# Window attention with a convolutional position term: a hand-ordered pipeline, interleaved convolution, 64x64 score tiles, GpSimd norms and a shared transposed buffer

## The chip, the cores and the metric

One core of one Trainium2 chip. The metric is device time in microseconds (us) of one execution. Both kernels give the reference's result within tolerance.

TensorE is called PE here, its weight loads PEld, VectorE DVE, ScalarE ACT, GpSimd POOL, and SyncE, which issues transfers, SP. "Clock" is the mean clock that the throttle granted to PE, 1.0 being full speed.

## The reference, cut to what matters

```python
# x: (1, 511, 511, 192) bf16; 7x7 windows: 73 x 73 = 5329 windows of 49 tokens; 4 heads of 48
pe = depthwise 3x3 convolution of x with dw_pe (per channel)
x0 = x + pe
h  = layernorm(x0)                       # no scale, no shift
qkv = windows(h) @ w_qkv                 # 192 -> 576
attn = softmax(q k^T * 48**-0.5)         # per window and head, 49 x 49
out = (attn v) @ w_o
return x0 + unwindow(out)
```

## The kernel before

Windows are taken in blocks of 128, one window to a partition (42 blocks), and within a block in 16 groups of 8 windows. The convolution treats one channel of a block as one matmul: the 81 pixels of the padded 9x9 patch are the contraction rows, the 128 windows the output partitions, the 49 tokens the columns. So a block has 192 convolution matmuls of 49 columns.

```python
def conv_tile(blk, it):                       # 20 channels in one tile of two PSUM banks, out of 4 tiles
    ps = PS.next()
    for cc in range(ncn):
        nc.tensor.matmul(ps[:, col : col + S], lhsT=XP[0:KP, :, c], rhs=T[0:KP, c, :], start=True, stop=True)
    nc.vector.tensor_tensor(out=xc[...], in0=ps..., in1=xc[...], op=ALU.add)      # x was loaded into xc
# ... (statistics with bn_stats, one token at a time; reciprocal root on DVE)
def transposes(blk):                          # layer norm's scale is folded into the transposing matmul
    D = Dcur.pop((blk, g))                    # ident * rstd, built on POOL
    nc.tensor.matmul(ps[0:KT, ...], lhsT=xc[:, s0 + ss, kt * KT : (kt + 1) * KT], rhs=D[:, ss, :], ...)
def stage_B(g):                               # scores: q holds both heads of a pair beside zeros
    for jj in range(4):
        for ab in range(2):
            for wp in range(2):
                nc.tensor.matmul(ps[64 * wp : 64 * wp + 64, col : col + 2 * S],
                    lhsT=k_[:, ab, w * S : w * S + 64], rhs=q_[:, ab, w, :, :]..., tile_position=(0, 64 * wp))
def proj(blk):
    # ... two matmuls of OT with Wo, then in every second tile the residual as an identity matmul:
    nc.tensor.matmul(ps[:, col : col + C], lhsT=ident[:], rhs=xc[:, s0 + ss, :], start=False, stop=True)
for g in range(NGL + LE + 1):                 # schedule of one group
    if ck == 0: transposes(blk)               # all 98 at once, at the start of a block
    stage_B(g - 1); stage_D(g - 2)
    if ck == LE: proj(blk - 1); store(blk - 1); load_xc(blk + 1)       # whole projection at once
    stage_E(g - 3)
    if ck >= CONV0: conv_tile(nb, ...)        # three tiles of 20 channels in one run, in four groups
    if ck == cend: load_xp(nb + 1)
    stage_A(g)                                # q, k, v of the group
```

KP is 81, KT 96 (half the channels), S 49. Stage A is q, k and v, B the scores and the exponential, D the weighted sum, E the transposition of its result.

## Time and profile before

Before: 5347.09 us (median of 2 runs, 5326.14 to 5368.04).

| | busy | share |
|---|---|---|
| PE | 4490 us | 84% |
| DVE | 3817 us | 72% |
| ACT | 2745 us | 51% |
| POOL | 758 us | 14% |
| granted clock | | 0.824 |

### The profile page before, as it was taken

How to read it: one execution, taken by the hardware profiler on the slowest of the kernel's cores; microseconds unless marked ns; L12 is line 12 of the kernel's file. 1: busy time of each engine (PE TensorE's matmuls, PEld its weight loads, DVE VectorE, ACT ScalarE, POOL GpSimd, SP SyncE). 2: the span in 40 equal slices, each digit the busy share in tenths (PEclk: the TensorE clock that was granted, in tenths of full speed). 3: DMA queues.
4: the chain of work that ended last, by engine and by line, in shares of the span. 5: the costliest groups of instructions: out<-in, count | busy, mean ns of one | idle time of the engine just before them, and what ended most of it. 6: DMA issues, size and time to landing. Idle time of an engine off the chain costs nothing.

```text
span 5337.2 us, 148265 instructions
## 1 busy us (share of the span) xinstructions
PE 4490.1 (84%) x65427; PEld 3661.5 (69%) x65427; DVE 3816.7 (72%) x6912; ACT 2744.5 (51%) x3385; POOL 758.0 (14%) x833
## 2 busy tenths in 40 slices
PE   2788888888888888888988888888888888888887
PEld 1666676667776676677776777767666776677776
DVE  6776777767776777777677777777777777767776
ACT  1554555545555555555555455555555555545555
POOL 1111111111111111111111111111111111111120
PEclk9887888887778887888788877788888888877888
DMA  6554445554455555554455544455555445544431
GB/s 67 51 75 70 68 71 80 82 73 68 68 68 70 71 72 74 71 74 71 68 73 91 75 68 68 68 72 72 74 72 72 73 70 78 85 74 67 68 48 32
DMA packets 512613, 375.27 MB, mean 70 GB/s; under 512 B 453129, under 2 KB 453321, under 8 KB 511958
## 3 DMA queue, kind: packets, MB, share of 16 engines
q1 hardware_dynamic: 480918, 265.08, 38.1%
q0 software_dynamic: 30592, 100.32, 10.6%
q8 instruction: 514, 8.42, 0.7%
q14 instruction: 141, 1.16, 0.1%
q10 hardware_dynamic: 448, 0.30, 0.0%
HBM read 265.31 MB, written 100.27 MB: 68 GB/s over the span
## 4 chain that ended last, share of the span: by engine, by line
PE 44%; DVE 16%; ACT 14%; DMA 12%; SPq 9%; issue 4%; POOL 1%; DVEq 0%; ACTq 0%; POOLq 0%
PE ps L412 12%; PE ps L282 8%; SPq L396 7%; DMA out_dram<-XC 7%; PE ps L369 6%; DMA XC<-in_x_dram 5%; PE ps L453 5%; PE ps L532 4%; DVE kT L424 4%; ACT hT L355 4%; DVE Qb L422 3%; PE ps L431 2%; DVE XC L284 2%; PE ps L560 2%; ACT kT L426 2%
## 5 line engine op out<-in xcount | busy, mean ns | idle before, releaser
L412 PE MATMUL ps<-hT,Wqk 96*128 96x392 bf16 x5336 | 1233.5, 380 | 76.7 <-DVE XC L284 62.2
L478 ACT ACTIVATE PT<-ps 128x784 bf16<-128x784 f32 x667 | 552.7, 829 | 1095.3 <-PE ps L453 1080.3
L421 ACT CAST Qb<-ps 64x784 bf16<-64x784 f32 x667 | 555.3, 833 | 657.5 <-PE ps L412 655.7
L412 PEld LDWEIGHTS <-Wqk 96*128 96x128 bf16 x5336 | 529.4, 108 | 486.1 <-issue 252.5
L284 DVE TENSOR_TENSOR XC<-ps,XC 128x980 bf16<-128x980 f32 x378 | 437.9, 1176 | 503.0 <-PE ps L282 247.2
L282 PE MATMUL ps<-T,XP 81*128 81x49 bf16 x8064 | 744.0, 264 | 55.5 <-DMA XP<-in_x_dram 55.5
L567 ACT CAST OT<-ps 96x784 bf16<-96x784 f32 x667 | 541.0, 811 | 456.0 <-PE ps L560 452.4
L282 PEld LDWEIGHTS <-XP 81*128 81x128 bf16 x8064 | 733.9, 220 | 57.6 <-issue 55.5
L431 PE MATMUL ps<-Wv,hT 96*128 96x192 bf16 x5336 | 663.5, 277 | 16.4 <-DVE On L544 9.0
L532 PE MATMUL ps<-V,PT 49*64 49x49 bf16 x21344 | 542.5, 195 | 159.1 <-DVE Qb L422 81.2
L431 PEld LDWEIGHTS <-hT 96*128 96x128 bf16 x5336 | 548.8, 111 | 180.0 <-issue 91.6
L544 DVE TENSOR_TENSOR On<-ps,rs 128x768 bf16<-128x768 f32 x667 | 634.6, 951 | 16.0
L532 PEld LDWEIGHTS <-PT 49*64 49x64 bf16 x21344 | 466.2, 116 | 260.4 <-issue 217.7
L327 POOL TENSOR_TENSOR D<-ident,rstd 128x896 bf16<-128x896 bf16 x294 | 486.2, 1681 | 1074.8 <-DVE rstd L320 1053.3
L424 DVE CAST kT<-ps 128x784 bf16<-128x784 f32 x462 | 450.0, 974 | 219.2 <-PE ps L412 209.1
L304 DVE BATCH_NORM_STATS2 bnst<-XC 128x6 f32<-128x192 bf16 x2058 | 600.5, 343 | 0.2
L453 PE MATMUL ps<-Qb,kT 128*64 128x98 bf16 x10672 | 408.0, 225 | 180.7 <-DVE Qb L422 132.2
L422 DVE CAST Qb<-ps 64x784 bf16<-64x784 f32 x462 | 451.6, 978 | 110.6 <-ACT Qb L421 100.1
L355 ACT CAST hT<-ps 96x896 bf16<-96x896 f32 x462 | 452.4, 1109 | 135.9 <-PE ps L346 134.9
L560 PE MATMUL ps<-ident,On 128*96 128x98 bf16 x5336 | 412.1, 226 | 114.4 <-DVE kT L424 110.9
L453 PEld LDWEIGHTS <-kT 128*64 128x64 bf16 x10672 | 341.5, 121 | 231.5 <-issue 131.7
L108 POOL DMA_DIRECT2D XC<-in_x_dram x386 | 216.0, 560 | 1865.9 <-DVE rs L543 996.3
(73 smaller groups left out, 4396.2 us busy)
## 6 DMA issues: line engine op xcount, KB each, us to landing
XC<-in_x_dram POOLq DMA_DIRECT2D x277, 294.0 KB, 7.5
out_dram<-XC SPq DMA_DIRECT2D x277, 294.0 KB
XP<-in_x_dram SPq DMA_DIRECT2D x210, 246.4 KB
XP<-in_x_dram SPq DMA_DIRECT2D x68, 243.0 KB
XC<-in_x_dram POOLq DMA_DIRECT2D x37, 165.4 KB, 7.1
out_dram<-XC SPq DMA_DIRECT2D x37, 165.4 KB
XP<-in_x_dram SPq DMA_DIRECT2D x22, 216.0 KB
XP<-in_x_dram SPq DMA_DIRECT2D x18, 212.6 KB
```

What stands on the lines that cost most here:

```text
L282: nc.tensor.matmul(ps[:, col : col + S], lhsT=XP[0:KP, :, c], rhs=T[0:KP, c, :], start=True, stop=True)
L304: nc.vector.bn_stats(out=bnst[:, s, :], in_=xc[:, s, :])
L355: nc.scalar.copy(out=hv[0:KT, kt, :, s0 : s0 + NDG], in_=src)
L412: nc.tensor.matmul(ps[:, ab * 512 : ab * 512 + TOK], lhsT=Wqk[kt][0:KT, which * 2 + ab, :], rhs=hT[0:KT, kt, ck * CH : (ck + 1) * CH, 0:S] ...
L421: nc.scalar.copy(out=dst[0:64, :, :, 0, :], in_=src[0:64])
L422: (nc.vector.tensor_copy if dve_help else nc.scalar.copy)(out=dst[64:128, :, :, 1, :], in_=src[64:128])
L424: nc.vector.tensor_copy(out=dst[:, :, 0:TOK], in_=two_bank(ps, TOK))
L431: nc.tensor.matmul(ps[:, col : col + C], lhsT=hT[0:KT, kt, ck * CH + 2 * jj : ck * CH + 2 * jj + 2, :].rearrange("p w s -> p (w s)"), rhs= ...
L453: nc.tensor.matmul(ps[64 * wp : 64 * wp + 64, col : col + 2 * S], lhsT=k_[:, ab, w * S : w * S + 64], rhs=q_[:, ab, w, :, :].rearrange("p ...
L478: nc.scalar.activation(out=pt[:, 0 : 16 * S].rearrange("p (b n) -> p b n", b=2), in_=two_bank(ps, 8 * S), func=ACTF.Exp, scale=scale,)
L532: nc.tensor.matmul(ps[64 * wp : 64 * wp + 64, col : col + S], lhsT=pt[64 * wp : 64 * wp + S, pc_ : pc_ + 64], rhs=v_[64 * wp : 64 * wp + S ...
L544: nc.vector.tensor_tensor(out=o_[:].rearrange("p (b j) (h d) -> p b (j h) d", b=2, d=DH), in0=ov[:, :, :, 0:DH], in1=r_[:].rearrange("p (b ...
```

## The change: intent and diff

The intent is to keep PE fed: no stage runs in a burst. The convolution is spread, a matmul or two after each long one, and is meant to hide its weight load there. Scores use four 64x64 tiles and q needs no zeros. Layer norm is applied ahead on GpSimd, so the transposes are plain; the residual too goes to GpSimd. The transposed norm (hT) and the transposed attention output (OT) share one buffer HO. The rows of x no longer sit in a buffer ahead of the convolution, but come in two small row buffers, on SP's queue. The core of a 1,367-line diff:

```diff
-    PS = _Rot([psum.tile([128, 1024], F32, name=f"ps{i}") for i in range(4)])
+    self.PS = _Rot([psum.tile([128, 1024], F32, name=f"ps{i}") for i in range(3)])
+    self.PE_ = psum.tile([128, 512], F32, name="pse")      # attention's transposes
+    self.PC = psum.tile([128, 512], F32, name="psc")       # convolution: ONE bank
 # ... convolution
-    ps = PS.next()                                         # 20 channels, then one add
+    PCB = self.PC
+    mm(PCB[:, (c % 10) * S : (c % 10 + 1) * S], lhsT=XP[0:KP, :, c], rhs=T[0:KP, c, :], ...)
+    if cv.c % 10 == 0 or cv.c == C:
+        nc.vector.tensor_copy(out=self.X[cv.b % 3][:, :, c0 : c0 + n], in_=PCB[...])
 # ... after each long matmul
+    def fill():
+        quota[0] += (conv_goal - conv_start) / nlong
+        while n and quota[0] >= 0.999 and conv.c < conv_goal:
+            quota[0] -= 1.0
+            conv_mm(conv)
 # ... x rows, norm, transposes
-    nc.gpsimd.dma_start(out=xc[...], in_=xw[...])          # whole block, POOL's queue
+    nc.sync.dma_start(out=t[p]..., in_=dram(x, *at))       # one of seven rows, SP's queue, two buffers
+    nc.gpsimd.tensor_tensor(out=hbuf(b)[:, s0:s1, :], in0=self.X[b % 3][:, s0:s1, :], in1=rstd..., op=ALU.mult)
+    for kt in range(2):                                    # both halves in ONE PSUM tile
+        for i in range(N): mm(pb[0:KT, kt * 1024 + i * 128 : ...], lhsT=h[...], rhs=ident[:], is_transpose=True)
+        eng = nc.vector.tensor_copy if kt == 0 else nc.scalar.copy
+        eng(out=HO[b % 2][0:KT, kt, :, s0 : s0 + N], in_=pb[0:KT, kt * 1024 : ...])
 # ... scores
-    nc.tensor.matmul(ps[...], lhsT=k_[:, ab, ...], rhs=q_[:, ab, w, :, :], tile_position=(0, 64 * wp))
+    mm(ps[...], lhsT=k_[64 * hp : 64 * hp + DH, ab, ...], rhs=q_[64 * hp : 64 * hp + DH, ab, ...], tile_position=(64 * hp, 64 * cp))
 # ... residual
-    nc.tensor.matmul(ps[...], lhsT=ident[:], rhs=xc[:, s0 + ss, :], start=False, stop=True)
+    nc.gpsimd.tensor_tensor(out=xv, in0=xv, in1=o[:, 0:n, :], op=ALU.add)
 # ... reload of the patches
+    if conv.c == C and xp_due:
+        load_xp(b + 2)
```

## The prediction

> **What bounds the kernel now.** I read the busy table, the costliest groups, the timeline of one block of 128 windows, the same block by stretches, and the DMA issues.

> ```profile
> PE 4490.1 (84%) x65427; PEld 3661.5 (69%) x65427; DVE 3816.7 (72%) x6912; ACT 2744.5 (51%) x3385; POOL 758.0 (14%) x833
> ...
> PEclk9887888887778887888788877788888888877888
> ```

> PE is the busiest engine, but its clock is granted at about 0.8, so "busy" holds slow time too. The stretches of one block (non-convolution steps, convolution steps, the next steps) show where; the columns are length, then busy time of PE, PEld, DVE, ACT, POOL, then the clock:

> ```profile
> 2016.00:2063.00 47.00, 40.12 (x695) 33.17 (x694) 36.41 (x44) 26.43 (x34) 4.42 (x8) 1.00 0.71 117
> 2064.00:2104.00 40.00, 38.98 (x419) 32.13 (x419) 22.95 (x27) 7.21 (x9) 1.00 (x4) 0.50 0.18 28
> ```

> Here the clock is full outside the convolution and half within it. The timeline of PE (start, length, operation) says what that costs:

> ```profile
> 2018.36 1.54 PE L412 MATMUL ps<-hT,Wqk 96*128 96x392 bf16 x8
> ...
> 2087.58 5.50 PE L282 MATMUL ps<-T,XP 81*128 81x49 bf16 x60
> 2092.91 2.79 PE L412 MATMUL ps<-hT,Wqk 96*128 96x392 bf16 x8
> ```

> The same eight q/k projections take 1.54 us at full clock and 2.79 us beside the convolution; 60 convolution matmuls take 5.50 us, 90 ns each (start to start also 90 ns in the few that ran at full clock[...]). A block takes (5337-157)/41.7 = 124 us, 157 us being where the first projection starts and 41.7 = 667 groups of 8 windows / 16.

> Groups that the sums below use (mean ns before the bar):

> ```profile
> L304 DVE BATCH_NORM_STATS2 bnst<-XC 128x6 f32<-128x192 bf16 x2058 | 600.5, 343 | 0.2
> L544 DVE TENSOR_TENSOR On<-ps,rs 128x768 bf16<-128x768 f32 x667 | 634.6, 951 | 16.0
> L327 POOL TENSOR_TENSOR D<-ident,rstd 128x896 bf16<-128x896 bf16 x294 | 486.2, 1681 | 1074.8 <-DVE rstd L320 1053.3
> L294 DVE TENSOR_TENSOR XC<-ps,XC 128x490 bf16<-128x490 f32 x42 | 28.1, 669 | 47.2 <-PE ps L282 47.2
> ```

> And a transfer that is hidden today: the SP queue's timeline in the same block.

> ```profile
> 2100.62 50.49 SPq L139 DMA_DIRECT2D XP<-in_x_dram  x27
> ```

> Reloading the patch buffer XP (10,332 packets of 384 B) keeps SP issuing for 50 us, and over all blocks takes 53 us on average. It starts when the convolution ends and has about 80 us until the next one, so nobody waits. Row loads of x go through another queue (POOL's) and land in 7.5 us.

> [...]The trace [...]shows a half clock also in a convolution stretch that is 97% busy (38.98 of 40.00)[...]. [...]wide transfers run at about 150 packets/us, stretches where several narrow ones overlap at up to 320. [...]the trace has 1681/896 = 1.9 ns an element in L327.

> **The change, part by part, for one block of 16 groups.**

> PE. Start-to-start at full clock, from the timeline: q/k 0.170 us, v and output projection 0.082, transposes of 128 columns 0.056. Unchanged: q, k, v: 16 x (8 x 0.170 + 8 x 0.082) = 32.3. Output projection 98 x 0.082 = 8.0; the 25 residual identity matmuls (25 x 0.085 = 2.1) go to GpSimd. Normalising ahead makes the 98 LN transposes plain: 98 x 0.056 = 5.5. Attention transposes widen from 98 to 128 columns: 16 x 8 x 0.056 = 7.2, from 5.8. Scores: 16 matmuls of 98 columns in about 0.47 us become 32 of 49 on four tiles; the output step's 32 of 49 take 0.63 us on two tiles. I take 0.5 us for each after: 16. Convolution: [...]I take 0.045 of the 0.090 us, 192 x 0.045 = 8.6. Sum 78 us, against some 88 before at full clock. The larger gain would be the clock: about 36% of the trace is at half clock, some 15 us a block that could go.

> First half of a block (convolution, groups 0 to 7, nine of 13 projection steps): 8 x (2.02 + 1.0 + 0.45) + 9 x 8 x 0.082 + 8.6 = 42 us of PE. But the convolution now has **one PSUM bank**, emptied after each ten channels; PE keeps order, so the eleventh stops all. Last matmul's drain 0.2 us, copy of 128x490 about 0.65 us (row L294), less one long matmul: 0.75 us, 20 times, a quarter of it where other PE work lies between: about 12 us. First half 54 us.

> Second half (LN of the next block) is **DVE's**: attention's reciprocal 0.256 + scaling 0.951 + transposed copy about 0.97 = 2.18, x 8 = 17.4; seven row adds of 1344 elements[...]: 5.3; 24 statistics of two rows, [...]0.54, 13; six and a part transposed copies of 1024 elements at 1.25 (128x896 takes 1.16): 7.7; reciprocal roots 1.4. Sum 45 us. PE then needs 37, ACT 37 (q, k, exp, v 3.26 x 8, projection copies 3, LN copies 8). Over the whole block DVE falls from 91 to about 76 us, ACT stays near 70 and POOL rises from 18 to about 45 (norms 9408 elements x 1.9 = 17.7; residual adds 9408 x 1.9 = 17.7; small ops): no bound alone.

> **The new wait that I expect.** All loads now go through SP in program order, and the row buffer holds two of seven rows. The reload of XP is issued at the end of group 7; row 3 of x is issued behind it, and its add stands first in group 10's DVE work, some two groups, 12 us, later. XP: 10,368 packets at 320/us = 32 us[...], start and landing 3 us: row 3 is there after 35 us. DVE, and with it PE, waits 35 - 12 = 23 us; I take 20. The last statistics, norm and transposes follow one another closely at the block's end: 3 us. Sum 54 + 45 + 20 + 3 = 122 us; less 3.5 because some of these waits overlap: 118.5. Start-up rises from 157 to about 200 us (convolution with one bank, rows behind XP, nothing beside). 200 + 41.7 x 118.5 = 5141, **about 5150 us**.

> **Rivals.**
> 1. Rows do not wait behind XP (or XP takes under 15 us): no 20 us, T = 98, 200 + 41.7 x 98 = 4290. For it: two halves of 64 windows on spread partitions, a layout that looks chosen for DMA. Against: [...]SP itself blocks while it issues.
> 2. [...]XP stays at 53 us, wait 41, T = 139, 6000. Against it: 320 packets/us is already reached in stretches.
> 3. The clock stays low: bank waits plus thin matmuls keep half clock in the first half, 42 becoming about 57: T = 133, 5750. For: such idling today in 2125 to 2135 after one 5.6 us stop. Against: the steady groups before idle 20% of the time (0.43 and 0.49 of 4.78 us) and keep full clock.
> 4. Bank waits are hidden and four tiles really run at once (B + D in 0.7 us): T about 103, 4500.

> **Range and chances.** The sum lies between rivals that pull by 600 to 850 us each way and of which more than one can hold. A hand-ordered redesign that spread its convolution so carefully was probably tuned, so I lean a little to the lower ones. 80% range 4550 to 5750. Faster by over 2% (under 5240) 0.56, within 2% 0.18, slower 0.26.

> **What would show each step right or wrong.** The clock row: mean over 0.9 if interleaving works, 0.8 or less if rival 3 holds. Waits of PE's convolution on the DVE copy: some 840 in all, 0.4 to 0.7 us each, about 500 us. Waits of the DVE row add on the x DMA: about one long one (20 us) a block, 41 in all, 800 us in total; the SP queue's XP issue about 30 us a block. Groups: scores and output together near 1.0 us per group; GpSimd norms and adds near 1.9 ns an element. If the row adds hardly wait, I am wrong towards 4300; if PE's convolution waits are several us each, towards 5800.

## More of the kernel before

The main lines stand in the prediction. Three more groups of PE matter later; they are from the view of groups of the kernel before, with contraction rows x columns behind the operation, then total and mean busy time, then PE's idle time ahead of them:

```profile
L412 PE MATMUL ps<-hT,Wqk 96*128 96x392 bf16 x5336 | 1233.5, 380 | 76.7 <-DVE XC L284 62.2 <-ACT hT L355 8.0 <-issue 5.2
L453 PE MATMUL ps<-Qb,kT 128*64 128x98 bf16 x10672 | 408.0, 225 | 180.7 <-DVE Qb L422 132.2 <-ACT kT L426 31.3 <-DVE kT L424 11.4
L377 PE MATMUL ps<-XC,ident 128*128 128x192 bf16 x1050 | 260.2, 248 | 0.0
```

The scores (L453) and the residual (L377) use all 128 contraction rows, though half of what the scores multiply is zeros. Both leave in the change.

## The result, and the profile after

After: **7374.32 us** (median of 2 runs, 7364.88 to 7383.76), 1.380 times before (95% interval 1.366 to 1.393). The prediction, 5150 us with a range up to 5750, was wrong in sign and far outside its range. Ratios here are not quite the ratios of the medians quoted. Executions over 1.5% slower than the fastest of the same kernel are left out of the means.

Busy rows and the clock row of the changed kernel's page (each digit a fortieth of the span, in tenths of full clock):

```profile
PE 5032.6 (68%) x75049; PEld 3971.4 (54%) x75049; DVE 2896.4 (39%) x4859; ACT 2853.6 (39%) x3521; POOL 1939.2 (26%) x2364
PEclk9866656665665666665656666555565655656557
```

DVE lost 920 us of work, as it should. PE is *less* busy in share, more in time, and its mean clock fell from 0.824 to 0.621. The stretches of one block (convolution; groups after it; one long stop; the rest; next convolution), columns as in the prediction:

```profile
3079.60:3159.50 79.90, 68.13 (x967) 56.09 (x968) 26.47 (x43) 32.81 (x41) 13.35 (x9) 0.53 0.08 19
3159.50:3180.00 20.50, 15.76 (x287) 12.10 (x286) 11.82 (x23) 11.35 (x15) 11.75 (x14) 0.75 0.52 131
3180.00:3198.00 18.00, 0.68 (x8) 0.53 (x7) 3.49 (x7) 1.54 (x2) 2.85 (x3) 0.54 0.72 189
3198.00:3250.00 52.00, 34.90 (x539) 25.67 (x538) 25.77 (x44) 21.80 (x27) 17.09 (x32) 0.70 0.10 28
```

The convolution stretch takes 80 us at a clock of 0.53; neither DVE nor ACT nor POOL is half busy there. In the third line everything stands still for 18 us. The view of waits names the releasers (total us, times, longest):

```profile
PE ps L371 <- DVE o L440: 977.7, 123, 64.9
DVE X L309 <- DMA xs<-in_x_dram: 902.5, 41, 67.1
PE psc L297 <- DVE X L302: 461.0, 716, 1.2
PE ps L350 <- DVE HO L359: 423.0, 294, 22.7
```

The first two are one stop seen from two engines: DVE's row add waits for a row of x, and PE then waits for attention's scaling, which stands behind it in DVE's order. The timeline of that stop:

```profile
3162.90 24.92 SPq L265 DMA_DIRECT2D XP<-in_x_dram  x18
3187.93 3.15 SPq L279 DMA_DIRECT2D xs<-in_x_dram  x4
3194.45 0.86 DVE L309 TENSOR_TENSOR X<-X,xs 128x1344 bf16<-128x1344 bf16 x1 [19.63 <-DMA xs<-in_x_dram]
3198.04 2.77 PE L371 MATMUL ps<-HO,Wqk 96*128 96x392 bf16 x8 [17.36 <-DVE o L440]
```

SP issues XP for 25 us, only then the row; the bracket gives the wait. And PE's timeline in the next convolution stretch, cut to the matmuls that had to wait for the one bank:

```profile
3253.08 0.20 PE L297 MATMUL psc<-T,XP 81*128 81x49 bf16 x1 [0.64 <-DVE X L302]
...
3257.43 0.20 PE L297 MATMUL psc<-T,XP 81*128 81x49 bf16 x1 [0.60 <-DVE X L302]
...
3259.95 0.20 PE L297 MATMUL psc<-T,XP 81*128 81x49 bf16 x1 [0.43 <-DVE X L302]
```

Each stop is short, but these follow one another by 4.4 and 2.5 us; 716 stops in 42 blocks are 17 in each convolution stretch, one every 4.7 us. Last, the groups of PE that answer to those of before:

```profile
L371 PE MATMUL ps<-HO,Wqk 96*128 96x392 bf16 x5336 | 1825.0, 478 | 992.8 <-DVE o L440 977.7 <-ACT HO L359 14.6
L409 PE MATMUL ps<-q,k 48*64 48x49 bf16 x21344 | 365.4, 212 | 22.6 <-ACT pO L469 8.3 <-ACT k L379 6.6
```

The same 5336 q/k matmuls cost 1825 us instead of 1234 with nothing in them changed. That is the clock and not the convolution matmuls between them: in a_all4 below, with the same interleaving at a mean clock of 0.925, they take 1254. The scores cost less (365 for 408 us), in matmuls of 48 contraction rows instead of 128.

To see where a block's time went, I took from each trace the median over blocks of the time from the first to the last convolution matmul (the convolution stretch, the prediction's first half) and from there to the next block's first (the rest). Medians do not add exactly.

| us per block | predicted | before | after |
|---|---|---|---|
| convolution stretch | 54 | 35.6 | 79.9 |
| rest | 64.5 | 87.7 | 90.7 |
| block period | 118.5 | 124.0 | 170.7 |

The excess over the prediction is 26 us in each half. 41.7 times 52.2 is 2177 us, which is nearly all of the 2224 us by which the total missed.

### The profile page after: what moved, and what is told of

Read it like the earlier page. It is cut to its first block, busy times and chain, and to the rows that moved or that the text cites. A ratio compares the mean times of both kernels' runs of the same rounds, so it can differ in the third digit from the quotient of the medians.

```text
span 7363.1 us, 168522 instructions
## 1 busy us (share of the span) xinstructions
PE 5032.6 (68%) x75049; PEld 3971.4 (54%) x75049; DVE 2896.4 (39%) x4859; ACT 2853.6 (39%) x3521; POOL 1939.2 (26%) x2364
## 4 chain that ended last, share of the span: by engine, by line
PE 52%; DVE 20%; SPq 16%; POOL 4%; issue 4%; DMA 3%; ACT 2%; DVEq 0%; POOLq 0%; ACTq 0%
PE ps L371 18%; SPq L265 14%; DVE X L302 6%; PE psc L297 6%; PE pse L453 6%; PE ps L387 6%; PE ps L350 6%; PE ps L465 6%; DVE HO L359 5%; DMA xs<-in_x_dram 3%; PE ps L430 3%; DVE HO L454 2%; DVE o L440 2%; POOL X L336 2%; PE ps L409 2%
## 5 line engine op out<-in xcount | busy, mean ns | idle before, releaser
L371 PE MATMUL ps<-HO,Wqk 96*128 96x392 bf16 x5336 | 1825.0, 478 | 992.8 <-DVE o L440 977.7
L297 PE MATMUL psc<-T,XP 81*128 81x49 bf16 x8064 | 1557.5, 238 | 494.4 <-DVE X L302 461.0
L473 POOL TENSOR_TENSOR X<-X,pO 128x768 bf16<-128x768 bf16 (+1 forms) x546 | 863.3, 1588 | 3306.3 <-ACT pO L469 3305.2
L297 PEld LDWEIGHTS <-XP 81*128 81x128 bf16 x8064 | 1337.0, 178 | 203.8 <-issue 114.1
L387 PE MATMUL ps<-Wv,HO 96*128 96x192 bf16 x5336 | 923.2, 303 | 35.3 <-ACT pO L469 35.3
L465 PE MATMUL ps<-Wo,HO 96*128 96x192 bf16 x4116 | 784.7, 328 | 3.6 <-ACT pO L469 2.9
L387 PEld LDWEIGHTS <-HO 96*128 96x128 bf16 x5336 | 588.9, 121 | 252.7 <-issue 217.0
L336 POOL TENSOR_TENSOR X<-X,rstd 128x1536 bf16<-128x1536 bf16 (+1 forms) x294 | 710.7, 2435 | 13.1
L465 PEld LDWEIGHTS <-HO 96*128 96x128 bf16 x4116 | 608.0, 176 | 180.9 <-issue 180.0
L417 ACT ACTIVATE pt<-ps 128x784 bf16<-128x784 f32 x667 | 550.3, 825 | 398.0 <-PE ps L409 396.0
L440 DVE TENSOR_TENSOR o<-ps,rs 128x768 bf16<-128x768 f32 x667 | 638.7, 958 | 23.4
## 6 DMA issues: line engine op xcount, KB each, us to landing
XP<-in_x_dram SPq DMA_DIRECT2D x64, 30.4 KB
```

What stands on the lines that cost most here:

```text
L297: mm(PCB[:, (c % 10) * S : (c % 10 + 1) * S], lhsT=XP[0:KP, :, c], rhs=T[0:KP, c, :], start=True, stop=True)
L336: nc.gpsimd.tensor_tensor(out=hbuf(b)[:, s0:s1, :], in0=self.X[b % 3][:, s0:s1, :], in1=rstd[:, i : i + n].unsqueeze(2).to_broadcast([128, ...
L371: mm(ps[:, ab * 512 : ab * 512 + TOK], lhsT=self.Wqk[kt][0:KT, which * 2 + ab, :], rhs=HO[b % 2][0:KT, kt, ck * CH : (ck + 1) * CH, 0:S], ...
L387: mm(ps[:, col : col + C], lhsT=HO[b % 2][0:KT, kt, w : w + 2, :].rearrange("p w s -> p (w s)"), rhs=self.Wv[kt][0:KT, :], start=(kt == 0) ...
L440: nc.vector.tensor_tensor(out=o_[:].rearrange("p b q (h d) -> p b (q h) d", d=DH), in0=ov[:, :, :, 0:DH], in1=r_[:].rearrange("p (b g) -> ...
L465: mm(ps[:, col : col + C], lhsT=HO[b % 2][0:KT, kt, :, s0 + i], rhs=self.Wo[kt][0:KT, :], start=(kt == 0), stop=(kt == 1))
```

## What the clock follows

What decides a window? I summed, for each window, columns times contraction rows / 128 over its matmuls ("rows fed"), and looked at the clock of the *next* window. From full clock, one limit sorts nearly all windows of a trace: above it the clock stayed, below it fell. The limit that sorts best is 3454 before (10 of 970 windows wrong) and 3289 after (12 of 440), in 3413 ns about 1.0 a ns; the expectations below use it so. Transposes are counted like other matmuls; without them 89 of 440 are wrong after. Counting columns alone sorts much worse (60 of 440 wrong after, at a limit of 5704 against 3136 before). Counting output columns too sorts better before and worse after (4 of 970, 31 of 440), so which of the two products the clock follows is open. Back from half clock the limit is similar but much less sharp (148 of 1631 wrong after, where the guess "never back" would be wrong in 238). This is a fit to records, not yet a cause.

A recount over all sixteen kept traces, those of the experiments below included, with one limit for all and each matmul counted where it starts, gives the same picture for the 14,339 windows at full clock. A limit of 3264 rows fed sorts all but 376 of them (before and after alone: all but 32 of 1411). Counting output columns too leaves 540 wrong, columns alone 1376, and the share of the window in which PE is busy 1406; the guess "the clock stays" is wrong in 3302. If the zero rows that some experiments add are left out of the count, 946 are wrong instead of 376.

The limit makes a claim that can be tried. Rows fed in all: 5.88 million before, 5.18 million after: the 64x64 scores feed 588 rows a group instead of 1568, and the residual's identity matmuls (4800 a block) are gone. At some 3290 rows per 3.413 us, a work of 5.18 million can hold the full clock throughout only if the kernel takes less than about 5.4 ms (an estimate from these numbers). A wait can push a window under the limit, and in the next PE is then slower: at half clock eight q/k matmuls took 2.79 us in the trace of before, at full clock 1.54.

## The experiments

| run | us (median) | ratio to before, 95% interval | clock |
|---|---|---|---|
| a_kpad | 6574.18 | 1.229 (1.223 to 1.234) | 0.831 |
| a_latexp | 6650.54 | 1.244 (1.239 to 1.248) | 0.637 |
| a_tr2 | 6859.24 | 1.283 (1.279 to 1.288) | 0.665 |
| a_bank | 6169.10 | 1.156 (1.152 to 1.161) | 0.751 |
| a_emove | 7403.83 | 1.384 (1.380 to 1.388) | 0.613 |
| a_burst | 7508.39 | 1.407 (1.403 to 1.410) | 0.681 |
| a_resid | 7367.11 | 1.380 (1.373 to 1.387) | 0.664 |
| a_all3 | 5569.99 | 1.040 (1.035 to 1.045) | 0.889 |
| a_all4 | **4862.68** | **0.909 (0.905 to 0.913)** | 0.925 |
| a_all4_burst | 5055.13 | 0.947 (0.944 to 0.949) | 0.933 |
| a_all4_dnorm | 5115.21 | 0.958 (0.954 to 0.963) | 0.910 |
| b_kpad | 5175.98 | 0.968 (0.964 to 0.972) | 0.899 |
| b_tiles | 5546.92 | 1.035 (1.029 to 1.041) | 0.762 |
| b_wide | 5122.96 | 0.957 (0.953 to 0.961) | 0.957 |

Names with a_ edit the kernel after, with b_ the kernel before. Before itself was 5340.9 to 5348.8 us in these batches. All were timed in rounds. The outputs are right. In the text "gains" are differences of medians to 7374 us. That figure comes from an earlier batch, and the batches ran on different chips; the kernel before, timed in each, differed by 0.15% between them.

### The clock: zero rows instead of idle rows

Theory C: the clock follows rows fed. Its rival W: waits alone explain the time, and the clock is their consequence. Feeding zeros in the unused contraction rows adds no instruction to PE (only five clearing ones to DVE, at the start) and changes no result.

```diff
# a_kpad (b_kpad is the same edit on the kernel before; there the scores have 128 rows already)
-  lhsT=self.Wqk[kt][0:KT, which * 2 + ab, :], rhs=HO[b % 2][0:KT, ...]      # 96 rows; v and projection alike
+  lhsT=self.Wqk[kt][:, which * 2 + ab, :],    rhs=HO[b % 2][:, ...]         # 128, zeros in 32
-  lhsT=XP[0:KP, :, c], rhs=T[0:KP, c, :]                                    # 81 rows
+  lhsT=XP[:, :, c],    rhs=T[:, c, :]
-  lhsT=k_[64 * hp : 64 * hp + DH, ...]                                      # 48 rows, q alike
+  lhsT=k_[64 * hp : 64 * hp + 64, ...]
```

> The changed kernel with the same instructions, but the contraction rows of the q/k, v, output-projection and convolution matmuls padded with zero rows to 128 (from 96 and 81) and of the scores to 64 (from 48). Theory C (clock): the granted clock of the next 3.41 us window follows from the rows fed to the array in this one (columns x rows / 128[...]), and most of the lost time is half clock; then rows fed per group of the convolution half rise from about 8100 to 10500 and the clock rises from 0.62 to 0.72 or more, time 6000 to 6800. Theory W (waits): time is lost in waits (row loads, one convolution bank, transposes) and the clock only follows idling; then nothing changes: 7374 within 1%, clock 0.62.

Measured 6574 us, 800 less, with the clock at 0.831. From a_kpad's page and its stretches (convolution, rest):

```profile
PE 4107.3 (62%) x75049; PEld 3383.8 (51%) x75049; DVE 2930.0 (45%) x4864; ACT 2835.3 (43%) x3521; POOL 1932.7 (29%) x2364
...
PEclk9888878878888888888878887888888887787878
```

```profile
2749.30:2813.30 64.00, 50.36 (x967) 44.96 (x967) 26.06 (x43) 32.62 (x41) 13.05 (x8) 0.92 0.10 24
2813.30:2902.80 89.50, 51.07 (x832) 37.28 (x830) 42.97 (x73) 34.87 (x44) 31.57 (x49) 0.73 0.33 84
```

PE has the same 75049 matmuls and 925 us less busy time; the convolution stretch fell from 79.9 to 63.0 us (median), and the clock in it, in the blocks shown, rose from 0.53 to 0.92. W is refuted: the rows fed take part in setting the clock, and rows of zeros count.

> The kernel before, with the same zero padding of the contraction rows to 128 (q/k, v, projection from 96, convolution from 81). Theory C: outside the convolution it is at full clock already, and a burst of convolution matmuls feeds only 49 columns in 90 ns, 0.54 a ns against the 1.0 a ns that the limit asks for, so the convolution steps stay at half clock; a few windows between recover: 5100 to 5340, clock 0.83 to 0.88. Theory W: 5347 within 1%.

Measured 5176 us, clock 0.899: 3.2% off the kernel before by the same edit. The time is in the expected range, the clock a little above it (0.83 to 0.88). So the clock follows the rows fed in the kernel before as well, not only in the change.

### The score tiles alone

```diff
# b_tiles: the kernel before with the score tiles of the change; q copied in as many pieces of the same size
-  lhsT=k_[:, ab, ...], rhs=q_[:, ab, w, :, :], tile_position=(0, 64 * wp)            # 16 matmuls, 128 rows, 98 columns
+  lhsT=k_[64 * hp : 64 * hp + DH, ...], rhs=q_[64 * hp : ...], tile_position=(64 * hp, 64 * cp)   # 32, 48 rows, 49 columns
```

> The kernel before with one part of the change alone: scores on four 64x64 tiles (48 contraction rows) in place of 128 zero-padded rows; the copies of q keep their number and size. Theory C: rows fed fall from 5.88 to about 5.23 million column-rows, the clock falls from 0.82 to 0.74-0.80, and the time stays or rises: 5350 to 5600, although the score step itself gets shorter by about 0.1 us a group (70 us in all). If the tiles were only good: 5280, clock 0.82.

Measured 5547 us, 3.5% slower than before, clock 0.762. The clock row and one group of b_tiles:

```profile
PEclk9677778777788777777877668768777786777778
```

```profile
L412 PE MATMUL ps<-hT,Wqk 96*128 96x392 bf16 x5336 | 1368.3, 410 | 88.7 <-DVE XC L284 60.2 <-ACT hT L355 14.8 <-issue 1.4
```

The q/k matmuls, which were not touched, cost 1368 us instead of 1234. The v matmuls went from 664 to 734 us, too; the convolution, which was at half clock already, stayed at 744. The scores themselves were not quicker either: 431 us against 408, in twice as many matmuls. So the score tiles, taken alone, lose, because most other steps run slower beside them.

### The residual back on PE

```diff
# a_resid: 49 identity matmuls a block back on PE, GpSimd's 546 adds out
-  mm(ps[...], lhsT=HO..., rhs=self.Wo[kt]..., start=(kt == 0), stop=(kt == 1))
+  mm(ps[...], lhsT=HO..., rhs=self.Wo[kt]..., start=(kt == 0), stop=False)
+  mm(ps[...], lhsT=ident[:], rhs=self.X[b % 3][:, s0 + i, :], start=False, stop=True)
-  nc.scalar.copy(out=o[...], in_=ps...); nc.gpsimd.tensor_tensor(out=xv, in0=xv, in1=o[...], op=ALU.add)
+  nc.scalar.copy(out=xv[...], in_=ps...)
```

> The changed kernel with one part undone: the residual is summed on PE again (49 identity matmuls of 192 columns and 128 contraction rows a block, 82 ns each at full clock) and GpSimd's 546 adds go. Theory 'rows' (the granted clock follows columns times contraction rows): 9408 rows a block more, 5.57 instead of 5.18 million in all, 7.6% more; zero padding added 24% and gave 800 us, so some 250 us pro rata, less up to 165 us for the matmuls themselves where PE does not wait: 7050 to 7330 us, clock 0.64 to 0.68. Theory 'work' (PE's time counts, the rows do not): 49 x 0.082 x 41.7 = 168 us more at full clock, about twice that at half: 7540 to 7710 us, clock 0.62.

Measured 7367 us, the same as after, between the two expectations; the clock, 0.664, is where 'rows' put it. The added rows came with a higher clock (q/k 1730 us instead of 1825), and the matmuls that brought them (589 us of PE) used the gain up. Moving the residual to GpSimd was neither gain nor loss here. Zeros in rows that stream anyway cost nothing in a_kpad (PE busy 4107 us with them, 5033 without, in 75049 matmuls each); added matmuls did cost.

### The one convolution bank

```diff
# a_bank: convolution alternates two banks; attention's transposes, whose bank it takes, use the rotating tiles
-  PCB = self.PC
+  PCB = (self.PC, self.PE_)[c // 10 % 2]
-  ebf = self.PE_[:].bitcast(BF)
+  ebf = PS.next()[:].bitcast(BF)[:, 0:1024]      # in stage E
```

> The changed kernel with two PSUM banks for the convolution alone. Theory W: the visible 461 us, so about 6910. Theory C: more, as in a_all3 to a_all4 (707 us), but with the rows unpadded the clock recovers only partly: 6700 to 6950, clock 0.63 to 0.68.

(It was built after a_all3 and a_all4, which come below.) Measured 6169 us, clock 0.751, a gain of 1205: the largest of all single edits, and far more than I had expected. The waits for the bank that it removes are only 461 us. One block of a_bank, convolution stretch and rest:

```profile
2563.40:2612.30 48.90, 46.85 (x966) 44.16 (x967) 26.00 (x43) 32.40 (x41) 13.01 (x8) 0.93 0.12 31
2612.30:2708.00 95.70, 55.59 (x833) 42.66 (x830) 42.91 (x73) 35.02 (x44) 31.61 (x49) 0.62 0.30 79
```

The convolution stretch fell from 79.9 to 49.5 us (medians) and its clock, in the blocks shown, rose from 0.53 to 0.93, with not a row more fed; the rest stayed (90.7 and 90.5). 30.4 us times 41 blocks is 1246, the whole gain. Some 0.6 us of idling (461 us in 716 waits) every 4.7 us was enough here to hold the stretch at 0.53, with rows as few as these.

The step from a_all3 to a_all4 is the same edit on a kernel whose zero rows already hold the clock up (0.889 over the span). The view of waits of a_all3:

```profile
PE psc L301 <- DVE X L306: 512.8, 716, 1.4
```

There the second bank removes about the same waits but gains only 707 us. What it gains beyond the waits is 194 us there and 744 us here. The other two edits of a_all3 leave the convolution stretch within about 1 us of after's 79.9 when they are run alone, so the difference is, as far as these runs show, what the clock adds to the price of the same stops.

But a_bank changes two things. The second, the move of attention's transposes, was run alone:

```diff
# a_emove: only the second of a_bank's two edits
-  ebf = self.PE_[:].bitcast(BF)
+  ebf = PS.next()[:].bitcast(BF)[:, 0:1024]
```

> The run with two convolution banks also moved the attention transposes out of their own single bank into the rotating three PSUM tiles, so its gain of 1205 us has two possible owners. This run does the move alone: the convolution keeps its one bank. Theory 'bank' (the second convolution bank is the cause): 7374 us within 3% (7150 to 7600), PE's convolution still waits about 460 us in some 700 waits on the DVE copy, clock 0.60 to 0.64. Theory 'move' (PE waited behind the transposes' single bank): 6100 to 6400 us, clock about 0.75. In between: both take part, in the proportion that the time shows.

Measured 7404 us, the same as after. From its view of waits:

```profile
PE psc L296 <- DVE X L301: 468.3, 716, 1.3
```

The bank's waits are as they were. The move alone gains nothing, so the 1205 us are the second bank's.

### The order of transfers

```diff
# a_latexp: reload the patches only when all seven rows of x are on their way
-  if conv.c == C and xp_due:
+  if conv.c == C and xp_due and n.loaded == WS:
```

> The changed kernel with the reload of XP issued only when all seven rows of x have been issued (three groups later). The DVE row add then no longer waits (902 us over 41 blocks before). Theory W: 6470, clock about the same. Theory C: at least as much, since 20 us less idling a block also leaves fewer windows at half clock: 6300 to 6500, clock 0.64 to 0.67. If XP then comes too late for the next convolution, a new wait of the first convolution matmul on XP shows, and the gain is smaller.

Measured 6651 us, a gain of 724 us; the clock hardly moved (0.637). I expected 6300 to 6500 with a clock of 0.64 to 0.67, a miss by 150 us: what I had hoped from the clock did not come. Its wait of DVE for x:

```profile
DVE X L309 <- DMA xs<-in_x_dram: 23.7, 1, 23.7
```

41 waits of 902 us became one of 24. The rest of a block fell from 90.7 to 73.6 us, the convolution stretch stayed at 80.1. The new wait that the expectation warned of is small: in all, the convolution waits for transfers 78 us in 5 cases instead of 32 us in one (149 us in 7 cases in a_all4).

### The shared transpose tile

The layer norm transposes write both channel halves into one PSUM tile; the second half's matmuls wait for DVE's copy of the first half (423 us in 294 waits in the view above). I had not foreseen this.

```diff
# a_tr2: a tile for each half
-  pb = PS.next()[:].bitcast(BF)           # ahead of the loop over halves
   for kt in range(2):
+      pb = PS.next()[:].bitcast(BF)
```

> The changed kernel with the two halves of an LN transpose unit in two PSUM tiles in place of one, so the second half's matmuls need not wait for DVE to have copied the first (423 us in 294 waits). Theory W: 423 us less, about 6950. Theory C: a little less than that, as most of the wait lies beside other waits: 7000 to 7250; the clock stays below 0.65.

Measured 6859 us, a gain of 515, more than the waits and more than expected (6950, or 7000 to 7250); the clock, 0.665, was to stay below 0.65. In a_tr2 this wait is nearly gone:

```profile
PE ps L349 <- DVE HO L358: 29.4, 26, 19.4
```

The rest of a block fell from 90.7 to 78.4 us.

### Together, and the version that beats both

a_all3 joins a_kpad, a_latexp and a_tr2; a_all4 adds a_bank's edits.

> The changed kernel with all three edits at once: zero rows to 128, XP reloaded after the rows of x, transposes in two PSUM tiles. The three alone took 800, 724 and 515 us off 7374; if they add up: 5335. Theory C says that they help each other, since less idling keeps more rows in each window: clock 0.88 or more, 5150 to 5335. If they overlap (each removes the same idle time): 5500 to 5800.

> The same with the convolution alternating between two PSUM banks (the attention transposes give theirs up and take a tile of the rotation). The waits of the convolution on its copy were 461 us in 716 waits. If they are on the path: 4750 to 4950. If other waits take their place (the rotation of three tiles now serves one more user): within 2% of a_all3.

Measured 5570 us (the third case, the gains overlap: 2039 singly, 1804 together) and, within the 4750 to 4950 expected, **4863 us**, 9.1% faster than before and 34% faster than after, with four small edits to the latter. The four gains singly add to 3244 us, together they are 2512. One block of a_all4 (convolution; the rest in three parts):

```profile
2130.40:2175.80 45.40, 43.95 (x967) 42.38 (x968) 26.07 (x43) 31.79 (x40) 13.05 (x8) 1.00 0.13 34
2175.80:2190.00 14.20, 9.95 (x195) 7.64 (x194) 11.19 (x16) 8.24 (x11) 4.57 (x4) 0.88 0.27 74
2190.00:2215.00 25.00, 16.83 (x332) 13.40 (x332) 19.47 (x34) 13.85 (x18) 18.39 (x25) 0.93 0.49 125
2215.00:2239.60 24.60, 15.99 (x309) 11.62 (x307) 12.92 (x23) 12.88 (x16) 9.64 (x21) 0.86 0.58 136
```

Now the convolution stretch is what the redesign meant it to be: PE 97% busy at full clock, 45.4 us. The rest still takes 64 us in which neither PE (42.8 busy) nor DVE (43.6) nor POOL (32.6) is full.

### Why the rest stays at 64 us

The timeline of a_all4 shows a chain at the end of each batch of statistics: reciprocal root, then the norm on GpSimd, then the transposes.

```profile
2222.94 5.46 POOL L339 TENSOR_TENSOR X<-X,rstd 128x1536 bf16<-128x1536 bf16 x2
2225.74 1.73 PEld L352 LDWEIGHTS <-X 128*96 128x96 bf16 x16 [5.71 <-POOL X L339]
2225.75 1.94 PE L352 MATMUL ps<-ident,X 128*96 128x128 bf16 x16 [5.48 <-POOL X L339]
```

PE waited 5.5 us for the norm here, and over the whole run:

```profile
PE ps L352 <- POOL X L339: 323.0, 84, 36.8
```

If this chain sets the rest, norms on DVE, which are quicker one by one (1.56 us against 2.43, as the run below shows), should shorten it.

```diff
# a_all4_dnorm
-  nc.gpsimd.tensor_tensor(out=hbuf(b)[:, s0:s1, :], ...)
+  nc.vector.tensor_tensor(out=hbuf(b)[:, s0:s1, :], ...)
```

> The four repairs, and the norms of layer norm moved from GpSimd to DVE. In the four repairs the stretch without convolution takes 64 us a block at nearly full clock though DVE is busy only 44 us there and I had predicted 45 for DVE as the bound; PE's largest wait is for GpSimd's norms (323 us in 84 waits). Theory 'chain' (statistics, root, norm, transposes in series, two norms of 2.7 us each on GpSimd being the longest link): the wait on the norm falls by half or more, the stretch to 58 to 60 us, 4600 to 4720 us in all. Theory 'DVE' (DVE's order of work sets the stretch, and it now gets ten us more a block): 4860 to 5150 us, stretch 64 to 72 us.

Measured 5115 us, 252 us slower; the rest grew from 63.9 to 70.7 us. Groups and waits of a_all4_dnorm:

```profile
L339 DVE TENSOR_TENSOR X<-X,rstd 128x1536 bf16<-128x1536 bf16 (+1 forms) x294 | 450.2, 1555 | 268.6 <-POOL rstd L331 268.6
```

```profile
PE ps L373 <- DVE o L442: 291.2, 55, 7.0
PE ps L352 <- DVE HO L361: 227.9, 44, 28.0
PE ps L352 <- DVE X L339: 218.3, 42, 35.6
```

The norms took 1.56 us each on DVE instead of 2.43 on GpSimd, but DVE got 10.8 us more a block and the period grew by 6.8. PE's wait for the norm fell by a third (323 to 218 us), not by half or more. The time is what theory 'DVE' said; that DVE's order of work weighs most in the rest is likely, but the chain is not ruled out, since this run made one link shorter and DVE's queue longer at once. Norms on GpSimd are a gain of 252 us in the repaired kernel: that part of the change was right. How the remaining 20 us of idling a block split up is open. One more candidate was not varied: q, k, v, the exponentials and the attention output have one buffer each in the changed kernel, where the kernel before had two or more.

### Is interleaving worth it, and is the convolution's cost its columns?

```diff
# a_burst, a_all4_burst: no convolution between long matmuls, a group's share runs at its end
-  while n and quota[0] >= 0.999 and conv.c < conv_goal:
+  while False and n and quota[0] >= 0.999 and conv.c < conv_goal:
```

> The changed kernel with the convolution matmuls of a group in one run at its end, not between long ones (one bank still). If the interleaving pays as meant: each convolution matmul costs 90 ns again, against about 70 between long ones at half clock, and the bank waits have no long matmul beneath: 8 us a block, 7700. If interleaving is what keeps the clock down (thin matmuls in every window), the other steps go back to full clock and it is faster: 6900 to 7200, clock over 0.65.

> The repaired kernel (a_all4) with the convolution in runs at the end of each group. Between long matmuls a convolution matmul costs 26 to 40 ns there, in a run 90: 192 x 55 ns = 10.5 us a block, 440 us; and a run of 27 feeds 0.54 columns a ns, under the limit, so some windows fall to half clock: 5300 to 5450, clock 0.85 to 0.90. If interleaving gained nothing: 4860.

Measured 7508 us (134 slower than after; clock 0.681) and 5055 us (192 slower than a_all4; clock 0.933). The first lies between the two expectations, the second is below what I expected. Interleaving is a gain in both, of 2 to 4%, and less than I had put on it in the repaired kernel. So the spreading of the convolution was not what made the change slow.

```diff
# b_wide: b_kpad, and each convolution matmul streams up to three channels' columns (147), two of them overwritten later
-  nc.tensor.matmul(ps[:, col : col + S], lhsT=XP[:, :, c], rhs=T[:, c, :], start=True, stop=True)
+  m = min(3, 10 - cc % 10, ncn - cc)
+  nc.tensor.matmul(ps[:, col : col + m * S], lhsT=XP[:, :, c], rhs=T[:, c : c + m, :], start=True, stop=True)
```

> b_kpad with each convolution matmul streaming three channels' taps (147 columns in place of 49; the two extra results are overwritten by the next matmuls), so that a burst feeds 147 columns in 90 ns. Nothing is removed, and 96 columns a matmul of useless work are added. Theory C: 1.6 a ns against the limit of about 1.0, the convolution steps go to full clock (0.95 or more over the span), 4600 to 4850. If the clock does not follow the rows fed: [...]5400.

Measured 5123 us against 4600 to 4850 expected: a miss. The clock went to 0.957, and the time fell by only 1% below b_kpad. Its timeline shows why:

```profile
2008.75 5.55 PE L287 MATMUL ps<-T,XP 128*128 128x147 bf16 x60
```

60 matmuls of 147 columns take 5.55 us, where before 60 of 49 took 5.50 at half clock. Within a run, a matmul starts some 90 ns after the one ahead of it at either clock (median in the trace of before: 90 ns in 549 cases at full clock, 89 in 7158 at half), and 147 columns took 92 where 49 took 90; what sets this pace was not shown. So the higher mean clock, 0.957 against b_kpad's 0.899, was worth only that 1%.

## Why the prediction was wrong

**The failed step: "First half 54 us", one half of the miss.** Its term for the single bank, "about 12 us", sized the waits rightly and their price wrongly. The waits were 461 us in 716 cases, 11 us a block (I had said about 500 in 840). But I let all other PE work of that half run at full clock, 42 us. It ran at 0.53, and the half took 79.9 us. With a second bank it takes 49.5 us, with the other repairs 45.3 at full clock. So 42 was nearly right for the work, and the one bank cost 30 us a block where I had 12: 11 in waits, and some 19 beyond them, most of it clock (a_all3 to a_all4, with the clock held up: 5 us a block beyond the waits).

**Rival 3 was the right one, mis-sized.** It said that bank waits plus thin matmuls would keep the clock low, and made of it 57 us and 5750 in all. I argued it down with steady groups of before that idle 20% of their time at full clock. That argument failed, since those groups feed more rows: their scores stream 1568 rows a group, the new ones 588. I counted idle time when I should have counted work. The profile of before held the hint, quoted in the prediction itself: half clock in a stretch that was 97% busy.

**"The larger gain would be the clock" had the wrong sign.** I saw the score tiles and the residual only as time saved on PE. The runs show: padded rows give 800 us back, and the score tiles alone make the kernel before 3.5% slower. The residual, put back alone, does not change the time. The sign for this stood in the prediction: a clock row of "0.8 or less if rival 3 holds"; it was 0.621.

**Right: the wait of x behind XP.** 20 us a block predicted, 22 measured (902 in 41), 17 us in the period when removed. The mechanism is the predicted one: in the block shown, row 3 was there 31.5 us after XP's issue began and was wanted after 11.9, where I had 35 and 12. Rivals 1 and 2 are thereby out: the rows do wait, and XP does not stay at 53 us (issue 25 us, predicted 32, before 50). What shortened the issue was not shown: the layout of the transfers, their number and what ran beside them all changed.

**Missed, in the other half: the shared transpose tile.** 423 us of waits, 515 us of time, 12 us a block in the rest. The code shows it (one tile, two halves, a copy between), and I did not read it so.

**Second half "45 us": right as a sum of DVE's work, wrong as a length.** DVE is busy 43.6 us in the rest of a_all4, yet the rest takes 64, 16 us more than the prediction's 45 + 3. Busy time of the busiest engine is only a lower bound of a half block in which three engines take turns. These 16 us and the 12 of the tile are the second failed step; together they are about the 26 us by which the rest missed.

**Small terms.** Start-up: 202 us until the first q/k matmul, predicted 200. GpSimd's norms: two of 1536 elements in 5.46 us in the timeline above, 1.8 ns an element where I took 1.9. None of these moved the outcome.

**What stays open.** Whether the clock follows contraction rows alone or rows times output columns (the recount favours the first, 376 against 540 wrong, but the second sorts some traces better); whether zeros count exactly as much as data (about so, by the recount); what decides the way back from half clock; and the last 20 us of idling in a_all4's rest.

## What to carry to other kernels

Before packing PE's work tighter, look at the granted clock and add up columns times contraction rows beside it: here work that left PE (5.88 to 5.18 million rows fed) went with a lower clock for all that stayed (0.824 to 0.621), and short PSUM waits then cost more than twice what the profile shows as waits (461 us shown, 1205 regained). In this kernel it paid to pad contraction rows with zeros where they stream anyway (800 us), to give a short chain of matmuls two banks (1205 us) and each copy its own tile (515 us), and to issue the small transfer that something waits for ahead of the large one (724 us). Do not count on more PE work to warm the clock: a_resid and b_wide raised it (0.621 to 0.664, 0.899 to 0.957) and gained nothing and 1%.
